# Moving k's copy from PSUM to SBUF from VectorE to ScalarE in the pairs of heads that run alone

## The chip, the cores and the metric

The kernel runs on one core of one Trainium2 chip. The metric is the device time of one execution in microseconds (us). "The profile" is a page made from the trace of one execution; busy times, waits and stretches are read from the same trace.

Engines in the profile: PE is TensorE's matmul, PEld its weight load, DVE is VectorE, ACT is ScalarE, POOL is GpSimd, SPq is the queue that issues DMA.

## The reference, cut to what matters

```python
# attention: q, k, v of shape (8, 12, 448, 64); then a gated feed-forward network on 3584 tokens
q_n, k_n = rmsnorm(q, g_q), rmsnorm(k, g_k)
scores = np.matmul(q_n, k_n.T) / np.sqrt(64)          # per batch and head
attn = softmax(scores)
x = (attn @ v) -> (3584, 768)
out = (silu(rmsnorm(x) @ w_gate) * (rmsnorm(x) @ w_val)) @ w_out    # weights arrive in float64
```

## The kernel before

Heads go two by two ("pairs", g = 0 to 47, six to a sequence). While the first sequence's attention runs (rounds g = 0 to 6) there is no feed-forward work to interleave, so those pairs "run alone"; in the same rounds the float64 weights are converted to float32 by a chain of ScalarE (split), VectorE (join, three instructions) and GpSimd (final addition). The first three functions below issue instructions, to each engine in the order of the program.

```python
def turn(g, i):                       # transpose q (i = 0) or k (i = 1) of pair g
    ...
    ps = (ps_m if todo else ps_f).tile([128, 512], F32, ...)
    for t in range(NT):
        nc.tensor.transpose(ps[:, t * P:(t + 1) * P], src[...], ident[0:P, 0:P])
    dst, flat = st["qkT", g][:, i, :], ps[:, 0:S]
    if i == 0:
        nc.scalar.activation(dst, flat, ACT.Copy, scale=gqk[:, 0:1])
    else:
        nc.vector.tensor_copy(dst, flat)

def score(g, cs):                     # 4 score tiles into 4 PSUM banks, then 4 exponentials
    ...
    nc.tensor.matmul(ps[0:P, 0:S], lhsT=qkT[r, 1, c * P:(c + 1) * P], rhs=qkT[r, 0, :], ...)
    ...
    nc.scalar.activation(e, ps[0:P, 0:S], ACT.Exp, scale=rs[:, n:n + 1])

def sums(g):                          # denominators; direct(g) is g <= NPAIR = 6
    ...
    terms = [[st["e", g, c, j] for j in range(2)] for c in range(NT)] if direct(g) else ...
    ... # matmuls of ones with the terms into den
    if direct(g):
        nc.vector.reciprocal(rd, den[:, 0:S])
    ...
    nc.vector.tensor_tensor(x, av[:, 0:S], rd, ALU.mult)     # frees the one PSUM bank of the values

for g in range(NG + 1):               # the rounds that run alone
    load_pair(g + 2)
    if g <= NPAIR:
        pe(lambda: score(g, (0, 1)))
        squares(g + 2, 0); squares(g + 2, 1)
        ...
        convert()                     # one turn of the weight conversion
        pe(lambda: turn(g + 1, 0)); pe(lambda: turn(g + 1, 1))
        if g: pe(lambda: values(g - 1))
        ...
        convert()
        if g: pe(lambda: sums(g - 1)); pe(lambda: score(g, (2, 3)))
        convert()
        continue
```

## Time and profile before

| | before |
|---|---|
| time, median of 3 (range) | 1632.63 us (1631.97 to 1633.83) |
| share of the span busy: PE, DVE, ACT, POOL | 99%, 54%, 31%, 39% |
| the copy in question, 128x448 from PSUM to SBUF on VectorE | 0.615 us; the change moves six of them |
| length of such a round | 11.32 us |

A PE that is 99% busy says little: in the round looked at below, the sixteen score matmuls keep PE busy for 4.30 us without a gap, and yet 0.85 us of it is the pace of the exponentials (4.23 us in the chain, where eight take 1.69 us elsewhere). What sets a round is read from the chain of waits and from the idle time in brackets at the end of a timeline row. The lines themselves are in the prediction.

### The profile page before, as it was taken

To read this page: it belongs to the slowest core of one execution; us is meant where nothing else is said; L and a number is where in the kernel's file an instruction comes from. 1 tells how busy PE (TensorE), PEld (TensorE's weight loads), DVE (VectorE), ACT (ScalarE), POOL (GpSimd) and SP (SyncE) were. 2 spreads that over 40 slices of the span, in tenths; PEclk is the share of its full clock that TensorE was granted. 3 is DMA by queue.
4 is the path that set the end of the run, shared out by engine and by line. 5 is a ranking of instruction groups with operands and counts; after the bars stand their busy time and mean duration, and the time that the engine had idled before them with its cause. 6 is when DMAs were issued, how large, how long until landed. Compare 5 with 4: busy or idle time off the path is not lost.

```text
span 1629.0 us, 21534 instructions
## 1 busy us (share of the span) xinstructions
PE 1607.8 (99%) x7352; PEld 1136.8 (70%) x7352; DVE 871.8 (54%) x1425; ACT 499.9 (31%) x975; POOL 632.7 (39%) x569
## 2 busy tenths in 40 slices
PE   7999999999999999999999999999999999999998
PEld 3444445678855888568875788658886587969984
DVE  6988998377842545435562354624565234433431
ACT  7756563232322332233233222322332123100110
POOL 6778777344433434244333333334353322100000
PEclk9999999999999999999999999999999999999999
DMA  7756674576865555565544755466454463557651
GB/s 202 223 165 200 188 225 146 163 231 203 264 191 168 155 156 150 175 189 158 159 118 125 206 154 154 120 211 188 140 158 126 148 193 109 151 182 238 174 149 45
DMA packets 249036, 276.83 MB, mean 170 GB/s; under 512 B 66644, under 2 KB 245844, under 8 KB 248916
## 3 DMA queue, kind: packets, MB, share of 16 engines
q1 hardware_dynamic: 248596, 275.34, 56.6%
q8 instruction: 61, 1.00, 0.3%
q14 instruction: 59, 0.48, 0.1%
q10 hardware_dynamic: 320, 0.00, 0.0%
HBM read 235.93 MB, written 39.32 MB: 169 GB/s over the span
## 4 chain that ended last, share of the span: by engine, by line
PE 91%; DVE 5%; DMA 2%; ACT 1%; SPq 0%; issue 0%; POOL 0%; DVEq 0%; ACTq 0%; POOLq 0%
PE ff L797 40%; PE ff L991 21%; PE sc L476 9%; PE av L501 9%; PE den L512 3%; PE ff L892 3%; PE ff L1022 2%; PE tr L461 2%; DVE top L646 1%; DVE top L644 1%; DVE rd L520 1%; DVE top L645 1%; ACT e L480 1%; DMA qk<-in_k_dram 1%; DMA raw<-in_moe_w_out_dram 0%; DMA raw<-in_moe_w_gate_dram 0%
## 5 line engine op out<-in xcount | busy, mean ns | idle before, releaser
L797 PE MATMUL ff<-x,w 128*128 128x224 f32 x1728 | 352.3, 354 | 0.8 <-DVE u L809 0.8
L797 PEld LDWEIGHTS ff<-x,w 128*128 128x128 f32 x1728 | 324.1, 190 | 12.1 <-issue 8.6
L797 PE MATMUL ff<-xs,w 128*128 128x224 f32 x1326 | 272.5, 353 | 0.4 <-DVE cc L809 0.4
L480 ACT ACTIVATE e<-sc,rs 112x448 f32<-112x448 f32 x384 | 211.9, 635 | 192.1 <-PE sc L476 187.0
L486 POOL TENSOR_TENSOR es<-e 112x448 f32<-112x448 f32 x82 | 95.2, 1181 | 437.3 <-ACT e L480 437.3
L797 PEld LDWEIGHTS ff<-xs,w 128*128 128x128 f32 x1326 | 248.7, 190 | 5.4 <-issue 4.7
L490 POOL TENSOR_TENSOR es<-es,e 112x448 f32<-112x448 f32 x164 | 186.0, 1145 | 85.5 <-ACT e L480 79.1
L991 PE MATMUL ff<-w,h 128*128 128x384 f32 x594 | 202.8, 487 | 0.0
L520 DVE RECIPROCAL rd<-rd 128x448 f32<-128x448 f32 x41 | 121.0, 2952 | 137.6 <-ACT rd L519 137.6
L476 PE MATMUL sc<-qkT 64*112 64x448 f32 x768 | 179.0, 570 | 3.9 <-ACT qkT L464 3.9
L991 PEld LDWEIGHTS ff<-w,h 128*128 128x128 f32 x594 | 111.5, 190 | 76.6 <-issue 2.7
L501 PE MATMUL av<-e,vt 112*64 112x448 f32 x768 | 154.9, 545 | 0.0
L444 POOL TENSOR_TENSOR rs<-ms,mhalf 112x16 f32<-112x16 f32 (+1 forms) x50 | 143.7, 2875 | 4.2
L476 PEld LDWEIGHTS sc<-qkT 64*112 64x112 f32 x768 | 69.0, 174 | 97.0 <-issue 71.0
L991 PE MATMUL ff<-w,so 128*128 128x384 f32 x338 | 117.3, 488 | 1.4 <-DVE y L952 1.4
L501 PEld LDWEIGHTS av<-e,vt 112*64 112x64 f32 x768 | 50.8, 136 | 95.3 <-issue 74.5
L1022 PE MATMUL ff<-x,w 128*128 128x448 f32 x288 | 112.0, 542 | 0.0
L809 DVE TENSOR_TENSOR cc<-ff,u 128x448 f32<-128x448 f32 x84 | 52.3, 623 | 93.4 <-PE ff L797 93.0
L991 PEld LDWEIGHTS ff<-w,so 128*128 128x128 f32 x338 | 63.2, 190 | 45.9 <-DVE y L952 2.6
L427 DVE TENSOR_REDUCE ms<-sq 112x8 f32<-112x512 f32 x96 | 61.2, 677 | 52.6 <-ACT sq L424 52.6
L1022 PEld LDWEIGHTS ff<-x,w 128*128 128x128 f32 x288 | 53.3, 190 | 50.9 <-issue 49.0
L682 POOL TENSOR_TENSOR w<-top,raw 128x384 int32<-128x384 int32 x72 | 78.5, 1105 | 25.1 <-DVE top L646 7.3
(101 smaller groups left out, 1693.9 us busy)
## 6 DMA issues: line engine op xcount, KB each, us to landing
w<-kept SPq DMA_DIRECT2D x479, 192.0 KB, 3.2
w<-kept_o SPq DMA_DIRECT2D x294, 192.0 KB, 2.7
kept<-w SPq DMA_DIRECT2D x89, 192.0 KB, 3.7
top<-kept SPq DMA_DIRECT2D x73, 192.0 KB, 3.2
qk<-in_q_dram SPq DMA_DIRECT2D x48, 224.0 KB, 3.7
qk<-in_k_dram SPq DMA_DIRECT2D x96, 112.0 KB, 3.5
vt<-in_v_dram SPq DMA_DIRECT2D x48, 224.0 KB, 2.8
raw<-in_moe_w_gate_dram SPq DMA_DIRECT2D x24, 384.0 KB, 4.6
```

Source lines behind the costliest of these rows:

```text
L427: nc.vector.tensor_reduce(out=ms[:, i * n:(i + 1) * n], in_=sq.rearrange("p (n d) -> p n d", d=D), axis=AX_X, op=ALU.add)
L444: nc.gpsimd.tensor_tensor(st["rs", g][:, cols], ms, mhalf[0:P, cols], ALU.pow)
L476: nc.tensor.matmul(ps[0:P, 0:S], lhsT=qkT[r, 1, c * P:(c + 1) * P], rhs=qkT[r, 0, :], start=True, stop=True)
L480: nc.scalar.activation(e, ps[0:P, 0:S], ACT.Exp, scale=rs[:, n:n + 1])
L486: nc.gpsimd.tensor_tensor(es, st["e", g, 0, j], st["e", g, 1, j], ALU.add)
L490: nc.gpsimd.tensor_tensor(es, es, st["e", g, c, j], ALU.add)
L501: nc.tensor.matmul(av[j * D:(j + 1) * D, 0:S], lhsT=vt[:, j, c, :], rhs=st["e", g, c, j], start=(c == 0), stop=(c == NT - 1))
L520: nc.vector.reciprocal(rd, rd)
L682: nc.gpsimd.tensor_tensor(data(key).bitcast(I32), top, lo, ALU.add)
L797: nc.tensor.matmul(bank[:, w * HT:(w + 1) * HT], lhsT=wt[:, c * 128:(c + 1) * 128], rhs=x[:, c, :], start=onto is None and w == c == 0, st ...
L991: nc.tensor.matmul(ps, lhsT=a, rhs=data(("wo", b, name, c)), start=first and c == 0, stop=c == NFP - 1, skip_group_check=True)
L1022: nc.tensor.matmul(bank[w][:, 0:S], lhsT=data(key)[:, c * 128:(c + 1) * 128], rhs=st["x", 0, half][:, c, :], start=half == c == 0, stop=ha ...
```

## The change

VectorE is busy for 9.6 to 11.1 us of a round of 11.32 us and ScalarE for 9.0. The intent is to relieve VectorE in those rounds by giving the plain copy of k's transposition to ScalarE, for the pairs 2 to 7, which are transposed in rounds 1 to 6.

```diff
         if i == 0:
             nc.scalar.activation(dst, flat, ACT.Copy, scale=gqk[:, 0:1])
+        elif 1 < g <= NPAIR + 1:
+            nc.scalar.copy(dst, flat)
         else:
             nc.vector.tensor_copy(dst, flat)
```

## The prediction

> **What bounds the kernel now.** I read the page first, then the chain of waits in order of time, then a table of stretches, then the timeline of one pair of heads, then the waits of VectorE and ScalarE.
>
> The page's summary and its chain line:
>
> ```profile
> PE 1607.8 (99%) x7352; PEld 1136.8 (70%) x7352; DVE 871.8 (54%) x1425; ACT 499.9 (31%) x975; POOL 632.7 (39%) x569
> PE 91%; DVE 5%; DMA 2%; ACT 1%; SPq 0%; issue 0%; POOL 0%; DVEq 0%; ACTq 0%; POOLq 0%
> ```
>
> TensorE carries 91% of the chain, VectorE 5%. So the first question is whether the few copies moved lie in that 5%. In the code the new branch holds for 1 < g <= 7, which is six pairs (2 to 7). Each is transposed one round of the loop early, so the six copies fall in rounds g = 1 to 6, about 24 to 86 us of the trace. The chain in order of time says what sets the pace there, and where VectorE first sets it:
>
> ```profile
> 64.34 4.23 PE sc L476 x16
> 68.57 0.92 PE tr L461 x8
> 69.49 3.16 PE av L501 x16
> 72.65 3.01 PE den L512 x16
> 75.66 4.23 PE sc L476 x16
> ...
> 125.05 0.80 PE den L512 x4
> 125.87 0.54 ACT rd L519
> 126.43 2.96 DVE rd L520
> ```
>
> From 23 to 125 us every piece of the chain is TensorE's. A round is 4.23 + 0.92 + 3.16 + 3.01 = 11.32 us, and it repeats to 0.01 us. VectorE's part of the chain starts at 126, forty microseconds after the last copy that the change touches. The stretches that are rounds of this loop (columns: PE, PEld, DVE, ACT, POOL busy, then clock and DMA):
>
> ```profile
> 30.33:41.65 11.32, 11.32 (x59) 4.70 (x57) 9.57 (x14) 9.04 (x18) 7.67 (x7) 1.00 0.73 213
> 64.27:75.59 11.32, 11.32 (x59) 4.70 (x57) 11.08 (x15) 9.03 (x18) 8.50 (x8) 1.00 0.72 210
> 86.90:101.09 14.19, 14.19 (x75) 6.29 (x73) 10.37 (x13) 7.96 (x16) 12.24 (x11) 1.00 0.65 201
> ```
>
> VectorE is almost full (11.08 of 11.32 us), which is surely why the change was thought of; ScalarE has 2.29 us over. But the rounds with VectorE at 9.57 and at 11.08 both last 11.32 us: VectorE's load doesn't set the length of a round. The timeline of one round shows how near it comes:
>
> ```profile
> 60.98 0.67 ACT L464 ACTIVATE qkT<-tr,gqk 128x448 f32<-128x448 f32 x1
> 61.50 0.62 ACT L532 ACTIVATE rd<-x 128x448 f32<-128x448 f32 x1
> 62.56 0.61 DVE L466 COPY qkT<-tr 128x448 f32<-128x448 f32 x1
> 64.27 4.30 PE L476 MATMUL sc<-qkT 64*112 64x448 f32 x16
> 64.46 2.96 DVE L516 RECIPROCAL rd<-den 128x448 f32<-128x448 f32 x1
> 65.31 2.21 ACT L480 ACTIVATE e<-sc,rs 112x448 f32<-112x448 f32 x4 [2.30 <-PE sc L476]
> 66.00 0.27 PEld L476 LDWEIGHTS sc<-qkT 64*112 64x112 f32 x2 [0.70 <-ACT e L480]
> 67.45 0.62 DVE L527 TENSOR_TENSOR x<-av,rd 128x448 f32<-128x448 f32 x1
> 69.42 3.23 PE L501 MATMUL av<-e,vt 112*64 112x448 f32 x16
> ```
>
> Three things are to be seen. The k copy ends at 63.17, and its first reader is the second half of the scores at 66.00, which waits for a PSUM bank that an exponential frees (the bracket). So the copy has 2.8 us of slack. Second, VectorE's only other hold on TensorE here is the single PSUM bank of the values: x ends at 68.07, the next values start at 69.42, so 1.35 us of slack. Third, the loss inside the round is the exponentials' pace: four PSUM banks of scores, so the second eight score matmuls follow the four exponentials. Eight take 1.69 us elsewhere in the chain, sixteen would take 3.38 and take 4.23, so 0.85 us a round. The change doesn't touch that.
>
> VectorE's and ScalarE's waits in 30 to 125 us, as groups (us in total, times, longest):
>
> ```profile
> DVE rd L516 <- PE den L512: 3.4, 3, 1.5
> DVE x L565 <- PE rb L558: 2.6, 1, 2.6
> DVE ms L548 <- PE msx L546: 1.1, 1, 1.1
> ```
>
> VectorE waits for TensorE here, and at 94 to 98 us (the last two lines) it runs dry, with 3.7 us of idle time. Any backlog from the rounds before is gone by then.
>
> [...] The trace has 615 ns for the VectorE copy and 525 ns mean for a ScalarE copy of the same shape out of PSUM (the later denominators), and ScalarE instructions in the round start 0.47 to 0.52 us apart[...]. [...] the trace mixes exponentials, squares, abs and scaled copies in these rounds at gaps of 0.44 to 0.52 us[...]. [...] one and the same conversion step (tensor_scalar, 128x384) lasts 0.35 us alone and 1.04 to 1.12 us beside a GpSimd operation. [...] Here VectorE is nearly saturated, but it is not what TensorE waits for.
>
> **The change part by part.**
> VectorE loses six copies: 6 x 0.615 = 3.7 us busy, 0.53 us of pitch each (62.56 to 63.09), all inside rounds of fixed length. On the path: 0. Part of it even comes back. In the round shown, the conversion step behind the copy would start at about 62.5[...]. So the reciprocal, which starts 0.19 us after the scores in the late rounds and 0.11 in the second, moves by at most 0.08 us, and x with it.
> ScalarE gains six copies of about 0.53 to 0.65 us, with 0.5 us of pitch: about 3 us in all. In program order each lies behind the scaled copy of q and the square of x, before the two splits of a weight piece. Its end would be near 62.6 in the round shown (61.97 + 0.6), half a microsecond before today's. In the earlier rounds (VectorE's copy at 38.39 and 49.70) it ends up to 1.1 us later, still over 3 us before use. The splits behind it move 0.5 us later; their readers come a whole conversion turn later, so nothing waits. ScalarE's idle time before the exponentials falls from 2.25 to 2.30 us to about 1.75 us, so the exponentials, which are on the path through the PSUM banks, start when they do now.
> TensorE: the scores' wait on VectorE becomes one on ScalarE, for an instruction older than the exponential that frees the bank and that the same matmul awaits anyway. No new wait.
> After 86 us nothing is changed in the program, and at 94 VectorE's state is the same as before. Sum on the path: 0.0 us in six rounds, with at most 0.1 us from the earlier x. Prediction 1632.5 us, which is the time before.
>
> **The rivals.**
> (a) VectorE is the bound in 30 to 91 us and all it sheds counts: 6 x 0.53 = 3.2 us, giving 1629.4. For it: 11.08 of 11.32 busy, and reciprocals that start with no idle time from 64 us on. Against: rounds of equal length at 9.57 and 11.08, and 1.35 us of slack at x. At pair 6, where no transposition lies between, x ends at 90.70 and the values start at 91.13; the slack is 0.43 but still there.
> (b) ScalarE becomes the bound: the copy delays the exponentials. It would have to eat 2.25 us of idle time with 0.5; if it did (a stall of a whole 0.6 us a round), 6 x 0.6 = 3.6 us, giving 1636.2. Against: the idle time in every one of the six rounds (3.78, then 2.25 to 2.30).
> (c) The relief reaches the stretch where conversions bind (126 to 233 us), because buffers come free earlier. That would be worth at most the 3.7 us shed, giving 1628.9. Against: the order of each engine is fixed by the program, VectorE runs dry at 94 to 98 us, and it waits 2.04 us again just before 126.43.
> [...]
>
> **Range and chances.** The three times of before span 1631.97 to 1633.83 us, so noise of about 1 us is larger than any expected effect. A tenth each for (a) and (c) in part and less for (b) widen it a little: 1630.2 to 1634.8. The largest rival is 3.7 us, 0.23%; 2% would be 33 us, nine times all that moves. Faster by over 2%: 0.005; within 2%: 0.99; slower: 0.005.
>
> **What would show it right or wrong.** In the changed profile: rounds of 11.32 us still, with scores of 4.23 in the chain; VectorE busy about 10.5 in the late rounds[...]; more idle time before the reciprocal; ScalarE about 9.5 busy and its idle time before the exponentials 1.7 to 1.8; the first chain piece of VectorE still near 126 us. A round of 10.8 us would prove (a); one over 11.5, with that idle time gone, (b); an unchanged mark at 125.05 with a shorter stretch to 233, (c).

## The result, and the profile after

| | before | changed |
|---|---|---|
| median of 6 runs | 1632.45 us | 1632.53 us |
| range | 1631.16 to 1634.62 | 1630.27 to 1633.18 |

The ratio is 0.9995, with a 95% interval of 0.9982 to 1.0008: the same time. (A ratio is the mean time of one kernel's fast runs over that of the other's of the same rounds, so not quite the ratio of the medians quoted.) The interval is -2.9 to +1.3 us. So the time alone speaks against rivals (a), (b) and (c) at their full size (-3.2, +3.6 and -3.7 us), but not against a part of them; for that the traces below are needed.

Line numbers behind 466 are two higher in the changed kernel: the scores are L478, the reciprocal L518, the copy of k on ScalarE is L466. The page's summary and chain lines of the changed kernel:

```profile
PE 1607.0 (99%) x7352; PEld 1136.7 (70%) x7352; DVE 873.7 (54%) x1419; ACT 502.7 (31%) x981; POOL 635.2 (39%) x569
PE 91%; DVE 5%; DMA 2%; ACT 1%; SPq 0%; issue 0%; POOL 0%; DVEq 0%; ACTq 0%; POOLq 0%
```

VectorE has six instructions fewer (1419 against 1425) and yet 1.9 us more busy time in this pair of traces (in a second pair, told below, it had 2.3 us less: 870.9 against 873.2). The chain's shares are unchanged. The chain in order of time, same columns as before (start, us, what):

```profile
73.96 4.24 PE sc L478 x16
78.20 0.92 PE tr L461 x8
79.12 3.16 PE av L503 x16
82.28 3.01 PE den L514 x16
```

The pieces of the round shown are as before to 0.01 us. The rounds as stretches (PE, PEld, DVE, ACT, POOL busy; clock, DMA):

```profile
28.54:39.86 11.32, 11.32 (x59) 4.69 (x57) 10.19 (x13) 9.48 (x19) 8.12 (x7) 1.00 0.78 211
62.49:73.89 11.40, 11.38 (x58) 4.68 (x56) 11.16 (x14) 9.49 (x19) 9.39 (x8) 1.00 0.71 212
```

ScalarE rose from 9.04 to 9.48 us. VectorE, one copy lighter, rose too: from 9.57 to 10.19 and from 11.08 to 11.16 us. The timeline of the round that answers to the one shown of before:

```profile
60.18 0.61 ACT L466 COPY qkT<-tr 128x448 f32<-128x448 f32 x1
60.44 1.61 POOL L535 TENSOR_TENSOR ss<-ss,rd 128x448 f32<-128x448 f32 x1 [1.66 <-ACT rd L534]
60.70 0.35 DVE L646 TENSOR_SCALAR top<-top 128x384 f32<-128x384 f32 x1
61.09 1.19 DVE L647 TENSOR_SCALAR top<-top 128x384 int32<-128x384 int32 x1
62.78 2.95 DVE L518 RECIPROCAL rd<-den 128x448 f32<-128x448 f32 x1
63.53 2.21 ACT L482 ACTIVATE e<-sc,rs 112x448 f32<-112x448 f32 x4 [1.81 <-PE sc L478]
65.77 0.62 DVE L529 TENSOR_TENSOR x<-av,rd 128x448 f32<-128x448 f32 x1
67.73 3.23 PE L503 MATMUL av<-e,vt 112*64 112x448 f32 x16
```

Three readings. ScalarE's idle time before the exponentials fell from 2.30 to 1.81 us and was not used up. The values' bank is free at 66.39 us and wanted at 67.73: 1.34 us of slack, as before. And the conversion steps, which now start where the copy was, meet GpSimd's addition: L647 took 1.19 us where it takes 0.36 in the next round (at 73.15 us), and the addition took 1.61 us where it took 1.14. That is where VectorE's freed time went in this trace; the reciprocal even began 0.29 us after the scores (62.78 against 62.49), where it was 0.19 before. The copy itself had never been stretched (0.610 to 0.625 us in all its instances up to 330 us); it ran inside the addition in the round shown of before (62.56 to 63.17 within 62.19 to 63.33) with neither of the two longer than elsewhere (0.61 and 1.14 us), and so had kept the conversion steps and the addition apart. VectorE's three conversion steps, summed over the five full rounds of the kernel before, as groups (busy us, mean ns, idle before):

```profile
L645 DVE TENSOR_SCALAR top<-top 128x384 int32<-128x384 int32 x15 | 11.0, 735 | 0.5
L646 DVE SCALAR_TENSOR_TENSOR top<-raw,top 128x384 int32<-128x384 int32 x15 | 9.2, 616 | 0.5
L644 DVE TENSOR_SCALAR top<-top 128x384 f32<-128x384 f32 x15 | 7.9, 529 | 0.0
```

The same three in the five full rounds of the changed kernel:

```profile
L647 DVE TENSOR_SCALAR top<-top 128x384 int32<-128x384 int32 x15 | 13.4, 893 | 0.5
L648 DVE SCALAR_TENSOR_TENSOR top<-raw,top 128x384 int32<-128x384 int32 x15 | 10.6, 707 | 0.5
L646 DVE TENSOR_SCALAR top<-top 128x384 f32<-128x384 f32 x15 | 7.7, 511 | 0.0
```

The same 45 instructions took 28.1 us before and 31.7 us after: 3.6 us more, against 3.1 us of copies shed in these five rounds. How much comes back differs from look to look: the second pair of traces gives 28.4 and 29.1 us. None of it matters for the end, because VectorE is not what TensorE waits for.

One difference between these two traces looks like a gain: the first piece of VectorE in the chain is at 124.75 us, where it was at 126.43. But the first full round began 1.79 us earlier, at 28.54 instead of 30.33, and the experiments show that to be chance.

### The profile page after: what moved, and what is told of

Same layout as the page of the kernel before. It is cut to its first block, busy times and chain, and to the rows that moved or that the text cites. A ratio compares the mean times of both kernels' runs of the same rounds, so it can differ in the third digit from the quotient of the medians.

```text
span 1628.5 us, 21528 instructions
## 1 busy us (share of the span) xinstructions
PE 1607.0 (99%) x7352; PEld 1136.7 (70%) x7352; DVE 873.7 (54%) x1419; ACT 502.7 (31%) x981; POOL 635.2 (39%) x569
## 4 chain that ended last, share of the span: by engine, by line
PE 91%; DVE 5%; DMA 2%; ACT 1%; SPq 0%; issue 0%; POOL 0%; DVEq 0%; ACTq 0%; POOLq 0%
PE ff L799 40%; PE ff L993 21%; PE sc L478 9%; PE av L503 9%; PE den L514 3%; PE ff L894 3%; PE ff L1024 3%; PE tr L461 2%; DVE top L648 1%; DVE rd L522 1%; DVE top L647 1%; DVE top L646 1%; DMA qk<-in_k_dram 1%; DMA raw<-in_moe_w_out_dram 0%; DMA raw<-in_moe_w_gate_dram 0%; ACT e L482 0%
## 5 line engine op out<-in xcount | busy, mean ns | idle before, releaser
L478 PE MATMUL sc<-qkT 64*112 64x448 f32 x768 | 178.2, 568 | 3.5 <-ACT qkT L464 3.5
L478 PEld LDWEIGHTS sc<-qkT 64*112 64x112 f32 x768 | 69.3, 174 | 96.1 <-issue 69.9
```

## The experiments

Twelve runs were made (e11 and e12 are the two kernels themselves once more), four at a time on one chip, each beside runs of the kernel before on the same chip. From every trace I took two marks: the start of the first full round (the scores of pair 1, second half, on PE) and "the mark", the start of VectorE's first reciprocal of the later pairs, which is on the chain. The span is the profiled one.

| run | round starts | mark | between | mark to end | median total | before, same chip |
|---|---|---|---|---|---|---|
| before | 30.33 | 126.43 | 96.10 | 1502.6 | 1632.45 | |
| changed | 28.54 | 124.75 | 96.21 | 1503.7 | 1632.53 | 1632.45 |
| e1 no reciprocal | 30.26 | 126.36 | 96.10 | 1502.3 | 1631.41 | 1631.83 |
| e2 VectorE +3 copies | 29.25 | 129.12 | 99.87 | 1503.1 | 1634.80 | 1631.83 |
| e3 ScalarE +3 copies | 31.82 | 128.96 | 97.14 | 1502.9 | 1633.69 (one run) | 1631.83 |
| e4 ScalarE +6 copies | 30.90 | 133.83 | 102.93 | 1503.3 | 1639.47 | 1631.83 |
| e5 short, before | 27.46 | 122.24 | 94.78 | 1503.4 | 1626.84 | 1632.00 |
| e6 short, changed | 31.23 | 125.67 | 94.44 | 1505.2 | 1629.26 | 1632.00 |
| e7 ScalarE to pair 13 | 29.79 | 125.91 | 96.12 | 1503.7 | 1631.45 | 1632.00 |
| e8 ScalarE in all pairs | 30.75 | 126.85 | 96.10 | 1502.2 | 1630.84 | 1632.00 |
| e9 loaded, before | 31.50 | 153.39 | 121.89 | 1502.9 | 1658.44 | 1631.64 |
| e10 loaded, changed | 31.56 | 152.72 | 121.16 | 1505.2 | 1657.60 | 1631.64 |
| e11 before again | 30.39 | 126.50 | 96.11 | 1503.3 | 1631.63 (one run) | 1631.64 |
| e12 changed again | 31.10 | 127.22 | 96.12 | 1503.2 | 1632.26 (one run) | 1631.64 |

The table separates the time into three parts: a start of 27 to 32 us that varies, the rounds between the two marks, and an end of 1502 to 1505 us that hardly depends on what happened before it.

**Does VectorE set the round?** e1 makes the reciprocals cheap. Its output is wrong, which doesn't matter for the time.

```diff
         if direct(g):
-            nc.vector.reciprocal(rd, den[:, 0:S])
+            nc.vector.tensor_copy(rd, den[:, 0:S])
```

> The kernel before, with VectorE's seven 2.96 us reciprocals of the pairs that run alone turned into plain copies of about 0.6 us (a wrong result on purpose). That takes 2.3 us a round off VectorE, four times what the change takes. My theory (VectorE is not waited for in these rounds): rounds stay at 11.3 us, the mark where VectorE's first reciprocal of the later pairs starts stays within about 2 us of 125 to 126 us, total within 1.5 us of before (1631 to 1634). Rival (a), VectorE is the bound: rounds of about 9 to 10 us, and 6 x 2.3 = 14 us or at least 8 us off the total.

Measured: 96.10 us between the marks, rounds of 11.31 and 11.32 us, total 1631.41 us, ratio 0.9996 (0.9980 to 1.0013). A late round as a stretch, columns as before:

```profile
64.20:75.51 11.31, 11.31 (x58) 4.69 (x57) 9.76 (x14) 9.03 (x18) 8.76 (x8) 1.00 0.71 222
```

VectorE's busy time fell from 11.08 to 9.76 us and the round stayed. Four times the relief of the change gives nothing either. Rival (a) falls.

**How much room has VectorE?** e2 loads it.

```diff
         else:
-            nc.vector.tensor_copy(dst, flat)
+            for _ in range(4 if 1 < g <= NPAIR + 1 else 1):
+                nc.vector.tensor_copy(dst, flat)
```

> The kernel before, with each of the six k copies made four times by VectorE (three extra, 0.53 us of pitch each, 1.6 us a round). My theory: VectorE's load of 9.6, 10.4, 10.9, 11.1, 11.1 us becomes 11.2 to 12.7, so it passes the round of 11.32 us and becomes the bound after the slack at the values' bank (1.35 us, 0.43 in the last round) is used: overflow about 0.7 + 1.2 + 1.4 + 1.4 us less that slack, 3 to 4.5 us later at the mark, and +2 to +4.5 us in the total (1634.5 to 1637). Rival (a): VectorE is the bound already, all of 6 x 1.6 = 9.6 us shows at the mark. A third possibility, VectorE has far more room than I read: nothing.

Measured: 3.8 us more between the marks and 3.0 us more in the median total (ratio 1.0018). By the trace TensorE now waits for VectorE in four of the six rounds (0.31 to 0.89 us), at the place that the prediction named, the values' bank:

```profile
70.46 3.23 PE L502 MATMUL av<-e,vt 112*64 112x448 f32 x16 [0.31 <-DVE x L528]
```

The sum came out, but not by my steps, so it was partly luck: steady rounds were 11.70 us, and copies that VectorE repeats into one place start 0.65 us apart, so the three extra ones cost 2.0 us a round (the four take 2.51 us until the next instruction starts, one takes 0.53), not 1.6. In a bound round of 11.70 us, VectorE's other work then takes about 9.7 us, though the profile of before showed it 11.08 us busy. The difference lies in two of the join steps, three of each a round: in a steady round of e2 the first took 0.351 us on average and the second 0.595, in the late round of before 0.646 and 0.830, together 1.6 us more.

**How much room has ScalarE?** e3 and e4 repeat the moved copy, four and seven times in all.

```diff
         elif 1 < g <= NPAIR + 1:
-            nc.scalar.copy(dst, flat)
+            for _ in range(4):     # e4: range(7)
+                nc.scalar.copy(dst, flat)
```

> The changed kernel, with each of the six k copies made four times by ScalarE (three extra at about 0.45 us of pitch, 1.35 us a round). ScalarE's idle time before the exponentials is 1.81 to 1.91 us in the changed kernel (2.26 in the first round). My theory: it falls to about 0.5 us, rounds stay 11.3 us, total as before. Rival (b), ScalarE is at its limit: rounds of 12.5 us or more and about 8 us in all.

Measured: rounds of 11.31 and 11.32 us, but two longer ones, 11.96 and 11.70 us; 1.0 us more between the marks. I had missed by a little. In the first of the longer rounds ScalarE had lost 0.76 us to two waits for its squares (0.22 and 0.54 us, the latter for a load of k), and repeated copies into one place start 0.56 us apart, not 0.45. So three extra copies, 1.7 us, take up nearly the whole slack of 1.85 us; 0.16 us of it was left in the other longer round. That one had a further cause: GpSimd's addition took 1.94 us instead of 1.14, and TensorE waited 0.32 us for the normalised q.

> The changed kernel, with each of the six k copies made seven times by ScalarE (six extra, about 2.7 us a round). My theory: this passes the 1.85 us of idle time by 0.85 us, so that the exponentials start late and TensorE waits: rounds of about 12.1 us, 4 to 5.5 us later at the mark, total +3 to +5.5 us (1635.5 to 1638). If ScalarE had more room than the idle time says: nothing. If the copies were on the path already: 6 x 2.7 = 16 us.

Measured: steady rounds of 12.67 to 12.69 us, 6.8 us more between the marks, total 1639.47 us (ratio 1.0046). Six copies at 0.56 us are 3.4 us; less the 1.85 us of idle time leaves 1.5, and 1.36 us a round were measured. TensorE waits in the second half of the scores:

```profile
70.68 2.58 PE L479 MATMUL sc<-qkT 64*112 64x448 f32 x8 [1.33 <-ACT e L483]
```

The kind of knee was right, its size was too small in both: in e4 because of the spacing, in e3 because of the spacing and of these waits. Rival (b) is real, but it starts at three more copies, not at one.

**Does the change pay where VectorE binds?** e5 and e6 shorten TensorE's part of the round in the kernel before and in the changed one. Their outputs are wrong, which doesn't matter for the times.

```diff
-        terms = [[st["e", g, c, j] for j in range(2)] for c in range(NT)] if direct(g) else ...
+        terms = [[st["e", g, c, j] for j in range(2)] for c in range(NT // 2)] if direct(g) else ...
```

> The kernel before, with half of the denominators' matmuls of the seven direct pairs left out (a wrong result on purpose): eight matmuls, about 1.5 us of TensorE less a round, a round of 9.8 us by TensorE alone. My theory: now VectorE, which wants up to 11.08 us a round, is the bound: the late rounds are about 10.8 to 11.1 us, not 9.8. The mark moves 3 to 5 us earlier, and the total by 1 to 4 us, since conversions and loads after the mark swallow part. If VectorE were not near its limit: rounds of 9.8 us and the mark 9 us earlier.

> The changed kernel, with the same half of the denominators' matmuls left out. My theory: here, where VectorE is the bound, the moved copy pays: late rounds shorter by 0.2 to 0.5 us than in the same cut of the kernel before, the mark 1 to 3 us earlier than there, the total 0.5 to 2.5 us below it. [...]

Measured for e5: rounds of 10.50, 10.50, 10.66, 10.73 and 11.12 us where TensorE's work alone asks for 9.8. From 26 to 70 us every piece of work in its chain is VectorE's, the k copy of 0.53 us among them. The mark came 4.2 us earlier, in the range; the total fell by 5.2 us, more than I gave: from the mark to the end it took 1503.4 us, so nothing behind the mark swallowed the gain. Measured for e6: the first two rounds were 9.81 and 10.08 us, so 0.69 and 0.42 us shorter than in e5; I had expected 0.2 to 0.5 us of the late rounds. The next three were 11.91, 11.14 and 13.19 us: a store of converted weights held ScalarE's next split, then GpSimd's chain from the squares to the normalised q came late, and TensorE's granted clock was 0.83 between 80 and 90 us. Its four totals span 1623.87 to 1632.74 us and their median lies 2.4 us above e5's, not below. As a comparison of the two copies this pair is inconclusive: in the shortened rounds other limits than VectorE come in.

**The same question with VectorE far above everything else.** e9 and e10 put 18 fills of an unused tile on VectorE behind each of the six k copies.

```diff
+        if i == 1 and 1 < g <= NPAIR + 1:
+            junk = tmp.tile([128, 160], F32, name="junk", tag="junk", bufs=1)
+            for _ in range(18):
+                nc.vector.memset(junk, 0.0)
```

> The kernel before, with 18 small fills of an unused tile (128x160) put on VectorE behind each of the six k copies. They touch no PSUM and read nothing, and cost an estimated 0.15 to 0.2 us each (one of 128x64 took 0.11), so 2.7 to 3.6 us a round, about twice the three extra copies of the earlier run, whose rounds were 11.70 us. My theory: VectorE is the bound, rounds of about 12.6 to 13.5 us, the total 6 to 11 us over before. It is one half of a pair: the question is what the moved copy is worth once VectorE binds.

> The changed kernel with the same 18 fills. My theory: here VectorE binds, so the moved copy pays what it costs: rounds shorter by 0.4 to 0.6 us than in the loaded kernel before, 2.5 to 3.5 us in all at the mark, and about as much in the total. [...] if GpSimd's own chain from the squares to the normalised q binds in the loaded rounds, the difference is under 0.2 us a round.

Measured: the fills lasted 0.19 us but started 0.29 us apart, so they cost 5.1 us a round and the kernels grew by 26.8 and 26.0 us, not 6 to 11. VectorE's reciprocals mark its rounds. VectorE's timeline of the loaded kernel before:

```profile
65.86 2.95 DVE L520 RECIPROCAL rd<-den 128x448 f32<-128x448 f32 x1
81.46 2.95 DVE L520 RECIPROCAL rd<-den 128x448 f32<-128x448 f32 x1
97.07 2.95 DVE L520 RECIPROCAL rd<-den 128x448 f32<-128x448 f32 x1
```

The same of the loaded changed kernel:

```profile
64.86 2.95 DVE L522 RECIPROCAL rd<-den 128x448 f32<-128x448 f32 x1
80.18 2.95 DVE L522 RECIPROCAL rd<-den 128x448 f32<-128x448 f32 x1
95.52 2.95 DVE L522 RECIPROCAL rd<-den 128x448 f32<-128x448 f32 x1
```

Rounds of 15.60 us against 15.32 to 15.34 us: here, where VectorE truly binds, the moved copy is worth about 0.28 us a round, not the 0.59 us that passed in e9 between its start and that of the first fill. Most of the rest went to the first join step: over three such rounds it took 3.0 us in the one and 3.7 us in the other, 0.24 us a round, which with 0.28 makes 0.52. My 0.4 to 0.6 was too high, and the 2.5 to 3.5 us at the mark did not come: it was 0.7 us earlier. The five rounds between the first six reciprocals of e10 were 0.27 to 0.41 us shorter than those of e9, but the last, from 110.84 to 127.88 us, took 17.04 us against 15.87. In it TensorE's value matmuls took 6.09 us, against 4.92 us in e9 and 3.23 us two rounds earlier in both (at 83.94 us in e10, 85.21 in e9), and VectorE then waited 5.86 us for TensorE, against 4.68. This pair shows the worth of the copy in a round, not in the total; the totals, 1658.44 and 1657.60 us, are too close to each other for their spread to add anything.

**Would the relief count later, where conversions are on the chain?** e7 and e8 widen the branch.

```diff
-        elif 1 < g <= NPAIR + 1:
+        elif 1 < g <= 2 * NPAIR + 1:     # e8: elif g > 1
```

> The changed kernel, with k's copy on ScalarE for six more pairs, 8 to 13, whose rounds lie in 101 to 260 us, where VectorE's conversions are on the chain. My theory: six copies of 0.54 us come off a chain that VectorE often sets, at most 3.2 us; loads of raw weights and ScalarE's own pieces of the chain give part back, so -0.5 to -2.5 us (1630 to 1632). The rival: the loads or ScalarE's order set the pace there, so 0 or up to +2 us.

> The changed kernel, with k's copy on ScalarE for every pair from 2 on. From 290 us on TensorE is busy throughout and both engines have room, so my theory expects the same as with the copies up to pair 13, within 1 us. A rival: in the later rounds ScalarE's copy comes behind an exponential or a tanh that waits for TensorE, and delays the transposition: +1 to +5 us.

Measured: 1631.45 and 1630.84 us against 1632.00, ratios 0.9997 (0.9984 to 1.0011) and 0.9993 (0.9979 to 1.0006). Neither differs from before, and the two lie within 1 us of each other, as expected of e8. But e7's interval is -2.6 to +1.8 us, so the times don't exclude a gain of the size that I gave. From the mark to the end e7 took 1503.7 us, no less than the kernels without the wider branch. So no gain from six copies less on VectorE was seen in a stretch where its conversions are on the chain; my 0.5 to 2.5 us are not shown. That stretch itself varies: from the mark to the fifth reciprocal behind it (at 271.40 us in before) it took 144.97 us in before, 146.06 in the changed kernel, 146.10 in e7 and 144.47 in e8; the second looks gave 145.66 for before and 145.52 for the changed kernel. Behind it the traces run in step: from there to a reciprocal at 1412.53 us before and changed take 1141.13 us each. What sets the spread was not taken apart; it stays open. No version with a right result beat both kernels clear of noise.

**Is the earlier start the change's doing?** e11 and e12 are the two kernels themselves, looked at again (no edit).

> The unchanged kernel before, looked at once more. In the two profiles of the case the first loaded round starts at 30.33 (before) and 28.54 us (changed), where the granted clock in 20 to 25 us was 0.66 and 1.00, before any moved copy runs. My theory: that is chance, not the change: the clock of this stretch differs between looks at one and the same kernel, and the time from the first loaded round to the mark is 96.1 us whatever it is. If the change had caused it, the clock here would be 0.66 again.

> The unchanged changed kernel, looked at once more. My theory: its clock in 20 to 25 us can be anything from 0.5 to 1.0, and from the first loaded round to the mark it takes 96.1 to 96.3 us, as the kernel before. If the change had caused the full clock, it would be 1.00 again.

The stretch of 20 to 25 us (the clock is the third number from the end) in the kernel before, first look:

```profile
20.00:25.00 5.00, 5.00 (x22) 2.29 (x24) 4.86 (x5) 4.72 (x10) 4.92 (x5) 0.66 0.31 55
```

The changed kernel, first look:

```profile
20.00:25.00 5.00, 4.98 (x30) 2.20 (x28) 4.87 (x5) 5.00 (x12) 4.76 (x5) 1.00 0.29 60
```

The kernel before, second look:

```profile
20.00:25.00 5.00, 4.88 (x20) 2.19 (x22) 4.88 (x5) 4.58 (x11) 4.92 (x5) 0.68 0.31 44
```

The changed kernel, second look:

```profile
20.00:25.00 5.00, 4.24 (x18) 1.92 (x19) 4.81 (x7) 4.51 (x10) 4.92 (x5) 0.66 0.33 58
```

The changed kernel had a clock of 1.00 in one look and 0.66 in the other, and its first full round began at 28.54 and at 31.10 us. e2, which is a kernel before with work added later, also had 1.00. The second look at the kernel before, 0.68, could not tell the two explanations apart; the 0.66 of the changed kernel and the 1.00 of e2 do. In the first look of the changed kernel the scores that begin at 19.68 us took 1.76 us, where those of before took 3.10, and the first moved copy came only at 25.83. So the 1.7 us are chance, and between the marks all four looks take 96.10 to 96.21 us. Over all fourteen traces the clock of this stretch was from 0.50 (e3) to 1.00: the first full round began at 27.46 to 29.25 us in the three with 1.00 (changed, e2, e5), and at 29.79 to 31.82 us in the eleven with 0.50 to 0.72. TensorE had been idle for 2.6 to 3.7 us just before or in this stretch in the four looks; the shortest of these waits, 2.64 us, was followed by 0.68 and one of 2.75 us by 1.00, and in e2 one of 3.58 us was followed by 1.00. In the loaded kernel before, waits of 2.49 and 4.27 us were followed by value matmuls of 4.86 and 4.92 us at a clock of 0.66 and 0.65, and one of 2.52 us by value matmuls of 3.23 us. So the length of the wait alone doesn't decide it; what does, these traces do not show.

## Why the prediction was right

The time (1632.53 us against 1632.5 predicted), the range and the mechanism all held. That the medians agree to 0.1 us is luck, since the runs of each kernel span about 3 us; the prediction was that nothing on the path moves, and that is what the traces show. By its steps:

- *The round is set by TensorE and the pace of the exponentials.* Held: 11.32 us before and after, and in e1 with the reciprocals gone. One round of the changed kernel was 11.40 us, when the stretched GpSimd addition made the normalised q late, a path to TensorE that the prediction named nowhere; in the second look all five were 11.31 or 11.32.
- *The k copy has 2.8 us of slack, x has 1.35 us.* Held: x's slack was 1.34 us in the changed kernel, and e2 shows TensorE waiting just there once VectorE is overloaded.
- *ScalarE's idle time falls to about 1.75 us.* It fell to 1.81 to 1.91 us, and from 3.78 to 2.26 us in the first round, where the clock differed too (0.66 and 1.00 in 20 to 25 us). In the second look it was 1.84 or 1.85 us in four rounds, 1.21 in one and 3.04 in the first. The copy lasted 0.57 to 0.61 us (median 0.581, against 0.525 on average for the later denominators of before), within the 0.53 to 0.65 given, and its follower started 0.41 us after it, not 0.5.
- *Part of VectorE's relief comes back.* Held, and it was larger than I said. I named one conversion step; over five rounds 3.6 us came back for 3.1 us shed. In the second look it was 29.1 us of steps against 28.4 in before again, so only 0.7 us. My reading is that the amount depends on how VectorE's steps happen to lie against GpSimd's additions (0.36 and 1.19 us for one and the same step); it was not taken apart further.
- *More idle time before the reciprocal.* Wrong in the first look (1.7 us in all, where before had 3.4), right in the second (5.3). It follows from the point above.
- *"VectorE is almost full (11.08 of 11.32 us)".* This reading was mis-sized. About 0.6 to 1.4 us of those 11.08 was not needed, an estimate from e2 and e9, which put VectorE's own need at 9.7 and 10.5 us (11.70 less 2.0, 15.60 less 5.1), and the first rounds of e5, with VectorE on the chain, took 10.50 us. It did not hurt the prediction, since it only made rival (a) look stronger than it was.
- *VectorE's first chain piece still near 126 us.* It was at 124.75 and 127.22 us, as the start varied (28.54 us at a clock of 1.00, 31.10 at 0.66). Measured from the first full round it moved by 0.1 us at most.
- *Rival (c), buffers come free earlier and help the conversion stretch.* From the mark to the end the two looks at before took 1502.6 and 1503.3 us, those at the changed kernel 1503.7 and 1503.2, so no run supports it; e7, which took VectorE's copies out of that stretch itself, showed no gain outside the noise.

## What to carry to other kernels

Busy time near 100% does not make an engine the bound (here 11.08 of 11.32 us, and the round stayed when 1.3 us of it went): ask which wait of the bounding engine would end earlier, and read its slack in microseconds before moving work. A busy figure can hold instructions that last longer beside another engine's work (here 0.36 and 1.19 us for the same step), so work taken off such an engine may be given back without a trace in the time (here 3.1 us shed and 3.6 us back in one pair of traces). And before you read a shift of one or two microseconds in a trace as the change's effect, find the first instruction that differs; here the shift came before it.
